# PSUM divided into two two-bank and four one-bank tiles in a packed-attention and squared-ReLU kernel

## The chip, the cores and the metric

The kernel runs on one core of a Trainium2 chip. The metric is the device time of one execution in microseconds (us). The core has five engines that run side by side, each through its own queue in order: TensorE (PE, matrix products), ScalarE (ACT), VectorE (DVE), GpSimd (POOL) and SyncE (SP, which here issues the stores). Matrix products are written into PSUM, an accumulator memory of eight banks; one bank holds 512 fp32 values in each of 128 partitions. ACT and DVE read PSUM and write the results to SBUF. Below, "to evict" a PSUM tile means to copy its values out of PSUM.

## The reference

There are 8 batches of 8 heads, 576 tokens, 64 values a head, and 32 packed queries. The attention is done twice, and its output goes through a feed-forward layer with a squared ReLU:

```
p_packed = softmax(p @ k^T / 8) @ v              # 32 packed rows per head
x        = softmax(q @ p_packed^T / 8) @ p_packed  # 576 rows per head
x        = x of all heads side by side           # (4608, 512)
h        = x @ w_in                              # (4608, 2048)
out      = relu(h)**2 @ w_out                    # (4608, 512), float32
```

## The kernel before

Work is cut by batch b (0 to 7), by quad qd of four heads (0, 1), by block fb of 128 of the 2048 hidden features (0 to 15), and by output tile t of 128 tokens (0 to 35). A batch has 576 tokens, thus four and a half output tiles. The steps of a batch are:

- **S1.b.0 and S1.b.1** (`s1`, L348): first scores of one quad, eight matmuls of 128x128 into one bank, then one exponential on ACT (`s1_exp`, L354). Both quads share one two-bank tile. **S1.b.2** (`s1_rest`, L357) holds what is left of both quads in the first bank of a second tile, `psr`.
- **PV.b.qd** (`pv`, L365): the packed values and the softmax sums, into the second bank of `psr`. **XT.b** (`pq_block`, `recip`, `extract`) takes them out of PSUM in small pieces on DVE and ACT, and only then is `psr` free.
- **M.b** (`m`, L398): the packed values times w_in, with 16 small matmuls for two chunks of 512 features. For b of 1 and above one M step takes two two-bank tiles at once; each is evicted in two pieces, one by ACT (L413) and one by DVE (L415).
- **S2.b.qd** (`s2`, L421): second scores, four matmuls of 288 columns into two banks, exponential on ACT (L431). **N.b.qd** (`n_sum`, L433): their sums, two matmuls, then logarithm and exponential on ACT and a product on DVE (L446).
- **F1.b.fb** (`f1_mm`, L450): four matmuls of 288 columns into a two-bank tile `ps_h`, ReLU on ACT (L465), square on DVE (L471) into `gT`, which holds two batches.
- **F2.t.fb** (`f2_mm`, L479): one matmul of 512 columns per fb, 16 of them accumulated into one bank for output tile t (L483). ACT or DVE then copies the bank to `o_sb` (`f2_out`, L497, helper `cast`, L260 and L262) and SP issues four stores. The even and the odd tile of a pair share one two-bank PSUM tile and one `o_sb` buffer.

The order of all instructions is written out by a planner (`Plan`, L47) that runs when the program is built. It knows the steps, their dependencies, a cost in us for each piece, a delay for a signal between engines (`HOPS`), and pools of slots. Each step takes slots before it starts and gives them back when a named piece ends. It books steps one after the other: the one that can start first goes first, with a small bias by stream, in which F2 comes last and F1 just before it. Each engine then gets its instructions in the order of the planned starts. On the chip, an engine whose next instruction waits does nothing else meanwhile.

The pool that matters is `"ps": 4`, four tiles of two banks, which are all of PSUM. S1, `psr`, M, S2, N, F1 and F2 all take from it. Waits for the tile's former use are put in by the framework when a tile is handed out again under the same tag, and also between instructions that use the same tile. The lines about F2 and its pool:

```
                if fb == 0 and t % 2 == 0:
                    take.append(("ps", 1))
...
                    if t % 2:
                        give.append(("ps", 1, f"F2.{t - 1}.0"))
                        give.append(("osb", 1, f"F2.{t - 1}.{fb}"))
...
                                lag=2.5 if fb == NFB - 1 and t % 2 else 0.0))
```

`lag` adds 2.5 us in the plan to the time at which the slots come free and at which the step counts as done. F1 of batch b depends on the last F2 step of the tiles of batch b - 2, since it writes over their half of `gT`.

Of the kernel before, what the change touches and what calls it, by code (L numbers as in the profile page):

```python
# [18 lines left out]
GM = 4  # L19
# [170 lines left out]
def kernel_impl(tc, q, k, v, p, w_in, w_out, out):  # L190
    nc = tc.nc
    B, H, S, Dh = q.shape
    assert Dh == D and S == JT * 32 and H == 2 * QH
    NQD = H // QH
# [9 lines left out]
    with ExitStack() as ctx:  # L204
# [2 lines left out]
        qkv = ctx.enter_context(tc.tile_pool(name="qkv", bufs=3))  # L207
        small = ctx.enter_context(tc.tile_pool(name="small", bufs=3))
        rpool = ctx.enter_context(tc.tile_pool(name="rpool", bufs=4))
        opool = ctx.enter_context(tc.tile_pool(name="opool", bufs=2))  # L210
        psum = ctx.enter_context(tc.tile_pool(name="psum", bufs=1, space=bass.MemoryType.PSUM))

        nc.scalar.preload_act_table_set("natural_log_exp_and_others")
# [20 lines left out]
        rD = [consts.tile([P, NQD], F32, name=f"rD{i}") for i in range(2)]  # L234
        gT = consts.tile([P, NFB, 2 * S], BF16, name="gT")

        def ps_tile(name, step, i=0):
            ps = psum.tile([P, 2, 512], F32, name=name, tag=f"ps{plan.slot['ps', step][i]}")
            for _ in range(plan.fill):
                nc.tensor.matmul(ps[:, 0, :256], lhsT=idle_b[:, :P], rhs=idle_b, start=True, stop=True)  # L240
            plan.fill = 0
            return ps

# [63 lines left out]
        class Att:  # L307
            def __init__(self, b):
                self.b = b
                self.v, self.vg, self.kT, self.pT, self.pq = v_b[b % NVB], v_g[b % 2], kT[b % NKT], pT_bd[b % NPT], pq_bd[b % 2]  # L310
                self.qT, self.a2, self.M = qT[b % 2], a2[b % 2], M[b % 2]
                self.e1, self.e1r, self.ppT, self.rD = e1[b % 2], e1r[b % 2], ppT[b % 2], rD[b % 2]
                self.kb, self.qb = {}, {}
                self.psm, self.pss, self.psn, self.e2, self.ls = {}, {}, {}, {}, {}

            def load_kq(self, nm, qd):
                t = getattr(self, nm + "b")[qd] = qkv.tile([P, JT * D], BF16, name=nm + "_b")
# [28 lines left out]
                    nc.tensor.matmul(ps, lhsT=kt[:, dh], rhs=self.pT[:, blk(qd, dh)], start=(dh == 0), stop=(dh == 1))  # L346

            def s1(self, qd):  # L348
                if qd == 0:
                    self.ps1 = ps_tile("ps_s1", f"S1.{self.b}.0")  # L350
                for g in range(GM):
                    self.s1_mm(self.ps1[:, qd, g * P:(g + 1) * P], qd, g)

            def s1_exp(self, qd):  # L354
                nc.scalar.activation(self.e1[:, qd], self.ps1[:, qd], ACT.Exp, scale=0.125)  # L355

            def s1_rest(self):  # L357
                self.psr = ps_tile("ps_pp", f"S1.{self.b}.2")
                for qd in range(NQD):
                    self.s1_mm(self.psr[:, 0, qd * P:(qd + 1) * P], qd, GM)  # L360

            def s1_rest_exp(self):
                nc.scalar.activation(self.e1r, self.psr[:, 0, :NQD * P], ACT.Exp, scale=0.125)

            def pv(self, qd):  # L365
                ps = self.ps_pp = self.psr[:, 1]

                def e1(g, i0, i1):
                    return self.e1[:, qd, g, i0:i1] if g < GM else self.e1r[:, qd, i0:i1]

                for pr in range(2):
                    h0 = qd * QH + 2 * pr
                    c0 = qd * P + pr * 64
                    for g in range(GM + 1):
                        nc.tensor.matmul(ps[:, c0:c0 + 64], lhsT=self.vg[:, g, h0 * D:(h0 + 2) * D],  # L375
                                         rhs=e1(g, pr * 64, pr * 64 + 64), start=(g == 0), stop=(g == GM))
# [98 lines left out]
        def tok(t):  # L475
            n0 = (t * P) % (2 * S)
            return slice(n0, n0 + P)

        def f2_mm(t, fb):  # L479
            if fb == 0:  # L480
                if t % 2 == 0:
                    po[t // 2] = ps_tile("ps_o", f"F2.{t}.0")
            nc.tensor.matmul(po[t // 2][:, t % 2], lhsT=gT[:, fb, tok(t)], rhs=w_out_b[:, fb, :],  # L483
                             start=(fb == 0), stop=(fb == NFB - 1))

        def o_tile(s):
            if s not in ob:
                ob[s] = opool.tile([P, 2, NE], F32, name="o_sb")
            return ob[s]

        def store(t, cols=slice(None)):
            for i in range(4):
                b, j = divmod(t * 4 + i, JT)
                dst = out[b * S:(b + 1) * S, :].rearrange("(a j) e -> j a e", j=JT)[j]
                nc.sync.dma_start(dst[:, cols], ob[t // 2][32 * i:32 * i + 32, t % 2, cols])

        def f2_out(t, eng):  # L497
            cast(eng, o_tile(t // 2)[:, t % 2], po[t // 2][:, t % 2])
            store(t)

        V, A, Q = nc.vector, nc.scalar, nc.gpsimd

        plan = Plan({"ps": 4, "kb": 3, "qb": 3, "v": NVB, "e2": 3, "r": 4, "osb": 2, "ls": 3, })
        T = [Att(b) for b in range(B)]
        QDS = range(NQD)
        NDV = 1
# [45 lines left out]
        def s1_steps(b):  # L552
            old = [f"PV.{b - 2}.1"] if b > 1 else []
            return [Step(f"S1.{b}.{qd}", [stage([("PE", 0.45, lambda qd=qd: T[b].s1(qd))]),
                                          stage([("ACT", 0.5, lambda qd=qd: T[b].s1_exp(qd))])],
                         [f"Tk.{b}.{qd}", f"X.{b}"] + old, [("ps", 1)] if qd == 0 else [],
                         [("ps", 1, f"S1.{b}.0")] if qd == NQD - 1 else []) for qd in QDS] + [
                    Step(f"S1.{b}.2", [stage([("PE", 0.23, T[b].s1_rest)]), stage([("ACT", 0.3, T[b].s1_rest_exp)])],
                         [f"Tk.{b}.{qd}" for qd in QDS] + [f"X.{b}"] + old, [("ps", 1)])]

        def pv_steps(b):
            old = [f"S2.{b - 2}.{qd}" for qd in QDS] + [m_of(b - 2, NFB - 1), m_of(b - 2, 0)] if b > 1 else []
# [10 lines left out]
                         [f"PV.{b}.1"] + old, (), [("ps", 1, f"S1.{b}.2")])]  # L573

        def g_steps(b):
            old = [f"PV.{b - 2}.1"] if b > 1 else []
# [5 lines left out]
        def m_steps(b):  # L582
            pairs = [(c,) for c in range(NWC)] if b == 0 else [(0, 1), (2, 3)]
            old = [f"F1.{b - 2}.{NFB - 1}"] if b > 1 else []
            return [Step(f"M.{b}.{cs[0]}",
                         [stage([("PE", 0.22 + 0.215 * len(cs), lambda cs=cs: T[b].m(cs))]),
                          stage(*[[("ACT", 0.6, lambda c=c, qd=qd: T[b].m_out(c, qd, A)),
                                   ("DVE", 0.67, lambda c=c, qd=qd: T[b].m_out(c, qd, V))] for c in cs for qd in QDS])],
                         [f"XT.{b}"] + [f"WI.{c}" for c in cs] + old, [("ps", len(cs))], [("ps", 1, None)])
                    for cs in pairs]  # L590

        def m_of(b, fb):
# [3 lines left out]
        def s2_steps(b):  # L596
            res = []
            for qd in QDS:
                res.append(Step(f"S2.{b}.{qd}", [stage([("PE", 0.49, lambda qd=qd: T[b].s2(qd))]),
                                                 stage([("ACT", 0.64, lambda qd=qd: T[b].s2_exp(qd))])],  # L600
                                [f"XT.{b}/1.{i}" for i in range(3)] + [f"Tq.{b}.{qd}"],
                                [("ps", 1), ("e2", 1)], [("ps", 1, None)]))
                res.append(Step(f"N.{b}.{qd}", [stage([("PE", 0.245, lambda qd=qd: T[b].n_sum(qd))]),
                                                stage([("ACT", 0.55, lambda qd=qd: T[b].n_ln(qd))]),
                                                stage([("ACT", 0.58, lambda qd=qd: T[b].n_inv(qd))]),
                                                stage([("DVE", 0.66, lambda qd=qd: T[b].n_mul(qd))])],
                                [f"S2.{b}.{qd}"] + ([f"F1.{b - 2}.{NFB - 1}"] if b > 1 else []), [("ps", 1), ("ls", 1)],
                                [("ps", 1, None), ("ls", 3, None), ("e2", 3, f"S2.{b}.{qd}")]))
            return [res[0], res[2], res[1], res[3]]

        def last_use(t):
# [4 lines left out]
        def f1_steps(b):  # L616
# [8 lines left out]
                         [("ps", 1), ("r", 1)], [("ps", 1, None), ("r", 2, None)]) for fb in range(NFB)]  # L625

        def f1_of(*ts):
            return sorted({t * P // S for t in ts} | {(t * P + P - 1) // S for t in ts})
# [1 line left out]
        def f2_steps(t):  # L630
            bs = f1_of(t)
            res = []
            for fb in range(NFB):
                segs = [stage([("PE", 0.2158, lambda fb=fb: f2_mm(t, fb))])]
                take, give = [], []
                if fb == 0 and t % 2 == 0:
                    take.append(("ps", 1))
                if fb == NFB - 1:
                    segs.append(stage([("ACT", 0.5, lambda: f2_out(t, A)), ("DVE", 0.59, lambda: f2_out(t, V))]))
                    if t % 2:  # L640
                        give.append(("ps", 1, f"F2.{t - 1}.0"))
# [75 lines left out]
```

## Time and profile before

| What | Value |
|---|---|
| Median of three runs | 283.61 us (283.16 to 284.52) |
| Profiled execution, its own time | 282.97 us |
| Span of its instructions | 281.2 us |
| PE busy | 236.8 us (84%) |
| ACT busy | 162.7 us (58%) |
| DVE busy | 149.9 us (53%) |
| POOL busy | 58.8 us (21%) |
| Granted TensorE clock, mean | 0.998 |
| F2 matmuls (L483) | 132.3 us busy |
| F1 matmuls (L454) | 72.6 us busy |
| M, S2 and N matmuls (L406, L425, L436) | 11.9, 11.4 and 6.2 us busy |
| Stores to `out` | 144 of 64 KB, 1.7 us to landing |

A profile lists when each instruction began and ended. PEld is the loading of weights into TensorE, which lies beside its matmuls. A row "A <- B: 8.4, 13, 0.7" among the waits says that an engine stood idle before instruction group A for 8.4 us in total, 13 times, 0.7 us at the longest, and that B was the last thing that it waited for. In the timeline a row gives start, duration, engine, line, operation, and in brackets the idle time of that engine just before it. Matmuls overlap one another, so the duration of a row of one matmul is longer than the distance between two of them. The profile records a few per cent of matmuls not at all, which makes some counts in rows too small.

### The profile page before, as it was taken

What the parts mean: (1) busy time and instruction counts of PE and PEld (TensorE: products, weight loads), DVE (VectorE), ACT (ScalarE), POOL (GpSimd) and SP (SyncE); (2) the same over time, 40 slices, a digit from 0 to 9 for tenths busy, and PEclk for the clock granted to TensorE, in tenths of its full rate; (3) what the DMA queues carried; (4) which work ended last, traced back from release to release, by engine and by line L of the source; (5) the groups of instructions that cost most, each with busy time, mean ns of one, the idle gap of its engine ahead of it and who ended that gap; (6) DMA issues with size and microseconds to landing.
All of it is one profiled execution on the core that took longest, in us unless ns stands there. A gap on an engine that the chain in (4) does not pass through costs nothing.

```text
span 281.2 us, 4890 instructions
## 1 busy us (share of the span) xinstructions
PE 236.8 (84%) x1812; PEld 134.4 (48%) x1840; DVE 149.9 (53%) x329; ACT 162.7 (58%) x304; POOL 58.8 (21%) x113
## 2 busy tenths in 40 slices
PE   0566688996979898978988998899899998988883
PEld 0523454654645565437633574366337545634341
DVE  5565898989988995557543184236506403700000
ACT  1237798978897655658862396458718515801110
POOL 8932643557467500000000000000000000000000
PEclk9999999999999999999999999999999999999999
DMA  6999999899999991211012200330131122023222
GB/s 94 178 206 208 203 205 196 150 177 158 212 220 222 221 207 53 59 37 40 0 40 65 65 23 1 76 77 0 37 77 37 28 63 61 1 70 80 57 61 69
DMA packets 26615, 28.37 MB, mean 101 GB/s; under 512 B 5600, under 2 KB 17888, under 8 KB 26592
## 3 DMA queue, kind: packets, MB, share of 16 engines
q0 software_dynamic: 19680, 18.62, 41.5%
q1 hardware_dynamic: 6912, 9.45, 13.5%
q8 instruction: 14, 0.23, 0.3%
q14 instruction: 9, 0.07, 0.1%
HBM read 37.22 MB, written 9.44 MB: 166 GB/s over the span
## 4 chain that ended last, share of the span: by engine, by line
PE 68%; DVE 13%; ACT 10%; issue 3%; DMA 3%; POOL 1%; ACTq 0%; DVEq 0%; POOLq 0%
PE ps_o L483 38%; PE ps_h L454 21%; DVE M L415 3%; ACT o_sb L260 3%; ACT M L413 3%; DVE qT L332 2%; PE ps_m L406 2%; DMA v_b<-in_v_dram 2%; PE ps_s L346 2%; PE ps_s L425 2%; PE ps_pp L375 2%; DVE kT L338 2%; DVE a L446 2%; DVE pq_bd L262 1%; ACT ls L443 1%
## 5 line engine op out<-in xcount | busy, mean ns | idle before, releaser
L483 PE MATMUL ps_o<-w_out_b,gT 128*128 128x512 bf16 x548 | 132.3, 379 | 13.8 <-ACT o_sb L260 8.4
L483 PEld LDWEIGHTS <-gT 128*128 128x128 bf16 x576 | 55.0, 98 | 76.3 <-issue 21.8
L471 DVE TENSOR_TENSOR gT<-r 128x576 bf16<-128x576 bf16 x128 | 57.1, 458 | 54.7 <-ACT r L465 47.9
L454 PE MATMUL ps_h<-a,M 128*128 128x288 bf16 x512 | 72.6, 290 | 5.6 <-DVE a L446 2.3
L465 ACT ACTIVATE r<-ps_h 128x576 bf16<-128x576 f32 x126 | 71.8, 676 | 9.4 <-PE ps_h L454 9.2
L454 PEld LDWEIGHTS <-M 128*128 128x128 bf16 x512 | 49.7, 99 | 24.7 <-issue 4.8
L260 ACT COPY o_sb<-ps_o 128x512 f32<-128x512 f32 x32 | 18.8, 587 | 60.6 <-PE ps_o L483 54.8
L413 ACT ACTIVATE M<-ps_m,rD 128x512 bf16<-128x512 f32 x41 | 26.0, 688 | 11.9 <-PE ps_m L406 9.3
L415 DVE TENSOR_SCALAR M<-ps_m,rD 128x512 bf16<-128x512 f32 x23 | 16.6, 747 | 19.4 <-ACT M L413 14.8
L332 DVE STREAM_TRANSPOSE qT<-q_b 128x1152 bf16<-128x1152 bf16 x16 | 21.7, 1366 | 0.5 <-DMA q_b<-in_q_dram 0.4
L323 POOL DMA_DIRECT2D v_b<-in_v_dram x32 | 20.0, 634 | 7.2 <-DMA w_in_b<-in_moe_w_in_dram 3.9
L346 PE MATMUL ps_s<-pT_bd,kT 128*128 128x128 bf16 x128 | 10.4, 230 | 11.5 <-DVE kT L338 9.9
L338 DVE STREAM_TRANSPOSE kT<-k_b 128x320 f32<-128x320 f32 (+1 forms) x32 | 18.7, 681 | 1.4 <-DMA k_b<-in_k_dram 1.3
L346 PEld LDWEIGHTS <-kT 128*128 128x128 bf16 x160 | 10.6, 103 | 15.0 <-DVE kT L338 13.5
L446 DVE TENSOR_TENSOR a<-e,ls 128x576 bf16<-128x576 bf16 x16 | 11.7, 749 | 10.8 <-ACT ls L443 10.7
L425 PE MATMUL ps_s<-qT,pq_bd 128*128 128x288 bf16 x64 | 11.4, 303 | 6.8 <-DVE pq_bd L262 3.7
L355 ACT ACTIVATE e<-ps_s 128x512 bf16<-128x512 f32 x16 | 9.4, 599 | 12.4 <-PE ps_s L346 12.3
L431 ACT ACTIVATE e<-ps_s,rD 128x576 bf16<-128x576 f32 x16 | 11.8, 742 | 6.0 <-PE ps_s L425 5.9
L440 ACT ACTIVATE ls<-ps_n 128x576 f32<-128x576 f32 x16 | 9.9, 648 | 6.1 <-PE ps_n L436 6.1
L406 PE MATMUL ps_m<-w_in_b,ppT 64*32 64x512 bf16 x256 | 11.9, 402 | 0.4 <-DVE M L415 0.2
L425 PEld LDWEIGHTS <-pq_bd 128*128 128x128 bf16 x64 | 6.1, 100 | 12.6 <-issue 4.6
L318 POOL DMA_DIRECT2D k_b<-in_k_dram x16 | 8.6, 544 | 13.5 <-DVE kT L338 10.8
(46 smaller groups left out, 128.5 us busy)
## 6 DMA issues: line engine op xcount, KB each, us to landing
out_dram<-o_sb SPq DMA_DIRECT2D x144, 64.0 KB, 1.7
k_b<-in_k_dram POOLq DMA_DIRECT2D x16, 288.0 KB, 6.6
q_b<-in_q_dram POOLq DMA_DIRECT2D x16, 288.0 KB, 7.4
v_b<-in_v_dram POOLq DMA_DIRECT2D x16, 160.0 KB, 6.4
v_b<-in_v_dram POOLq DMA_DIRECT2D x16, 128.0 KB, 6.6
w_in_b<-in_moe_w_in_dram POOLq DMA_DIRECT2D x4, 512.0 KB, 10.3
w_out_b<-in_moe_w_out_dram POOLq DMA_DIRECT2D x8, 256.0 KB, 9.0
p_b<-in_p_dram POOLq DMA_DIRECT2D x1, 192.0 KB, 10.0
```

The costliest lines, as they stand in the source:

```text
L260: nc.scalar.copy(dst, src)
L323: nc.gpsimd.dma_start(self.v[i:P:4, :, :n * D], v[self.b].rearrange("h (a j) d -> a h (j d)", j=JT)[:, :, J0[i] * D:(J0[i] + n) * D])
L332: nc.vector.transpose(self.qT[:, qd].rearrange("p dh (j a) -> p j dh a", a=32), self.qb[qd][:].rearrange("p (j dh dl) -> p j dh dl", dh=2, ...
L338: nc.vector.transpose(self.kT[:, qd, :n * P].rearrange("p (g a jp) -> p jp g a", jp=4, a=32)[:, i:i + 2], self.kb[qd][:, J0[i] * D:(J0[i] ...
L346: nc.tensor.matmul(ps, lhsT=kt[:, dh], rhs=self.pT[:, blk(qd, dh)], start=(dh == 0), stop=(dh == 1))
L413: nc.scalar.activation(dst, self.psm[c][:, qd], ACT.Copy, scale=self.rD[:, qd:qd + 1])
L415: nc.vector.tensor_scalar_mul(dst, self.psm[c][:, qd], self.rD[:, qd:qd + 1])
L425: nc.tensor.matmul(ps[:, c], lhsT=self.pq[:, blk(qd, dh)], rhs=self.qT[:, qd, dh, c * HALF:(c + 1) * HALF], start=(dh == 0), stop=(dh == 1))
L454: nc.tensor.matmul(ps[:, c], lhsT=a.M[:, qd, fb * FB:(fb + 1) * FB], rhs=a.a2[:, qd, c * HALF:(c + 1) * HALF], start=(qd == 0), stop=(qd = ...
L465: nc.scalar.activation(Att.cols(r), ph[a.b, fb], ACT.Relu)
L471: eng.tensor_tensor(out=g_of(a.b, fb), in0=r, in1=r, op=ALU.mult)
L483: nc.tensor.matmul(po[t // 2][:, t % 2], lhsT=gT[:, fb, tok(t)], rhs=w_out_b[:, fb, :], start=(fb == 0), stop=(fb == NFB - 1))
```

## The change

The pool `ps` of four two-bank tiles becomes two pools: `p2`, two tiles of two banks, and `p1`, four tiles of one bank. M, S2, N and F1 take from `p2`. Each quad of the first scores, `psr` and each output tile take one tile from `p1`. The rest of the first scores and the packed values now lie in the same bank one after the other, where they had a bank each. An M step of two chunks takes both `p2` tiles. Each output tile has its own `o_sb` buffer: four buffers of one tile, where there were two buffers of two. The lag of 2.5 us now stands behind every output tile, and each gives back its slots itself. No costs and no stream priorities are changed, and the planner makes a new order from the new pools.

```diff
-        opool = ctx.enter_context(tc.tile_pool(name="opool", bufs=2))
+        opool = ctx.enter_context(tc.tile_pool(name="opool", bufs=4))
...
-        def ps_tile(name, step, i=0):
-            ps = psum.tile([P, 2, 512], F32, name=name, tag=f"ps{plan.slot['ps', step][i]}")
+        def ps_tile(name, step, i=0, pool="p2"):
+            ps = psum.tile([P, 2, 512] if pool == "p2" else [P, 512], F32, name=name,
+                           tag=f"{pool}_{plan.slot[pool, step][i]}")
...
             def s1(self, qd):
-                if qd == 0:
-                    self.ps1 = ps_tile("ps_s1", f"S1.{self.b}.0")
+                ps = self.ps1[qd] = ps_tile("ps_s1", f"S1.{self.b}.{qd}", pool="p1")
...
             def s1_rest(self):
-                self.psr = ps_tile("ps_pp", f"S1.{self.b}.2")
+                self.psr = ps_tile("ps_pp", f"S1.{self.b}.2", pool="p1")
...
             def pv(self, qd):
-                ps = self.ps_pp = self.psr[:, 1]
+                ps = self.ps_pp = self.psr
...
             if fb == 0:
-                if t % 2 == 0:
-                    po[t // 2] = ps_tile("ps_o", f"F2.{t}.0")
-            nc.tensor.matmul(po[t // 2][:, t % 2], lhsT=gT[:, fb, tok(t)], rhs=w_out_b[:, fb, :],
+                po[t] = ps_tile("ps_o", f"F2.{t}.0", pool="p1")
+            nc.tensor.matmul(po[t], lhsT=gT[:, fb, tok(t)], rhs=w_out_b[:, fb, :],
...
-                ob[s] = opool.tile([P, 2, NE], F32, name="o_sb")
+                ob[s] = opool.tile([P, NE], F32, name="o_sb")
...
-        plan = Plan({"ps": 4, "kb": 3, "qb": 3, "v": NVB, "e2": 3, "r": 4, "osb": 2, "ls": 3, })
+        plan = Plan({"p2": 2, "p1": 4, "kb": 3, "qb": 3, "v": NVB, "e2": 3, "r": 4, "osb": 4, "ls": 3, })
...
-                         [f"XT.{b}"] + [f"WI.{c}" for c in cs] + old, [("ps", len(cs))], [("ps", 1, None)])
+                         [f"XT.{b}"] + [f"WI.{c}" for c in cs] + old, [("p2", len(cs))], [("p2", 1, None)])
...
-                if fb == 0 and t % 2 == 0:
-                    take.append(("ps", 1))
+                if fb == 0:
+                    take.append(("p1", 1))
...
-                    if t % 2:
-                        give.append(("ps", 1, f"F2.{t - 1}.0"))
-                        give.append(("osb", 1, f"F2.{t - 1}.{fb}"))
-                    else:
-                        take.append(("osb", 1))
+                    give += [("p1", 1, f"F2.{t}.0"), ("osb", 1, None)]
+                    take.append(("osb", 1))
...
-                                lag=2.5 if fb == NFB - 1 and t % 2 else 0.0))
+                                lag=2.5 if fb == NFB - 1 else 0.0))
```

More of the change, by code (lines that the diff above doesn't have):

```diff
@@ L235, in kernel_impl @@
         gT = consts.tile([P, NFB, 2 * S], BF16, name="gT")
-        def ps_tile(name, step, i=0):
-            ps = psum.tile([P, 2, 512], F32, name=name, tag=f"ps{plan.slot['ps', step][i]}")
+        def ps_tile(name, step, i=0, pool="p2"):
+            ps = psum.tile([P, 2, 512] if pool == "p2" else [P, 512], F32, name=name,
+                           tag=f"{pool}_{plan.slot[pool, step][i]}")
             for _ in range(plan.fill):
-                nc.tensor.matmul(ps[:, 0, :256], lhsT=idle_b[:, :P], rhs=idle_b, start=True, stop=True)
+                nc.tensor.matmul(ps[:, 0, :256] if pool == "p2" else ps[:, :256], lhsT=idle_b[:, :P], rhs=idle_b, start=True, stop=True)
             plan.fill = 0
@@ L313, in __init__ @@
                 self.kb, self.qb = {}, {}
-                self.psm, self.pss, self.psn, self.e2, self.ls = {}, {}, {}, {}, {}
+                self.psm, self.pss, self.psn, self.e2, self.ps1, self.ls = {}, {}, {}, {}, {}, {}
             def load_kq(self, nm, qd):
@@ L348, in s1 @@
             def s1(self, qd):
-                if qd == 0:
-                    self.ps1 = ps_tile("ps_s1", f"S1.{self.b}.0")
+                ps = self.ps1[qd] = ps_tile("ps_s1", f"S1.{self.b}.{qd}", pool="p1")
                 for g in range(GM):
-                    self.s1_mm(self.ps1[:, qd, g * P:(g + 1) * P], qd, g)
+                    self.s1_mm(ps[:, g * P:(g + 1) * P], qd, g)
             def s1_exp(self, qd):
-                nc.scalar.activation(self.e1[:, qd], self.ps1[:, qd], ACT.Exp, scale=0.125)
+                nc.scalar.activation(self.e1[:, qd], self.ps1[qd], ACT.Exp, scale=0.125)
             def s1_rest(self):
-                self.psr = ps_tile("ps_pp", f"S1.{self.b}.2")
+                self.psr = ps_tile("ps_pp", f"S1.{self.b}.2", pool="p1")
                 for qd in range(NQD):
-                    self.s1_mm(self.psr[:, 0, qd * P:(qd + 1) * P], qd, GM)
+                    self.s1_mm(self.psr[:, qd * P:(qd + 1) * P], qd, GM)
             def s1_rest_exp(self):
-                nc.scalar.activation(self.e1r, self.psr[:, 0, :NQD * P], ACT.Exp, scale=0.125)
+                nc.scalar.activation(self.e1r, self.psr[:, :NQD * P], ACT.Exp, scale=0.125)
             def pv(self, qd):
-                ps = self.ps_pp = self.psr[:, 1]
+                ps = self.ps_pp = self.psr
                 def e1(g, i0, i1):
@@ L494, in store @@
                 dst = out[b * S:(b + 1) * S, :].rearrange("(a j) e -> j a e", j=JT)[j]
-                nc.sync.dma_start(dst[:, cols], ob[t // 2][32 * i:32 * i + 32, t % 2, cols])
+                nc.sync.dma_start(dst[:, cols], ob[t][32 * i:32 * i + 32, cols])
         def f2_out(t, eng):
-            cast(eng, o_tile(t // 2)[:, t % 2], po[t // 2][:, t % 2])
+            cast(eng, o_tile(t), po[t])
             store(t)
         V, A, Q = nc.vector, nc.scalar, nc.gpsimd
-        plan = Plan({"ps": 4, "kb": 3, "qb": 3, "v": NVB, "e2": 3, "r": 4, "osb": 2, "ls": 3, })
+        plan = Plan({"p2": 2, "p1": 4, "kb": 3, "qb": 3, "v": NVB, "e2": 3, "r": 4, "osb": 4, "ls": 3, })
         T = [Att(b) for b in range(B)]
@@ L555, in s1_steps @@
                                           stage([("ACT", 0.5, lambda qd=qd: T[b].s1_exp(qd))])],
-                         [f"Tk.{b}.{qd}", f"X.{b}"] + old, [("ps", 1)] if qd == 0 else [],
-                         [("ps", 1, f"S1.{b}.0")] if qd == NQD - 1 else []) for qd in QDS] + [
+                         [f"Tk.{b}.{qd}", f"X.{b}"] + old, [("p1", 1)], [("p1", 1, None)]) for qd in QDS] + [
                     Step(f"S1.{b}.2", [stage([("PE", 0.23, T[b].s1_rest)]), stage([("ACT", 0.3, T[b].s1_rest_exp)])],
-                         [f"Tk.{b}.{qd}" for qd in QDS] + [f"X.{b}"] + old, [("ps", 1)])]
+                         [f"Tk.{b}.{qd}" for qd in QDS] + [f"X.{b}"] + old, [("p1", 1)])]
         def pv_steps(b):
@@ L572, in pv_steps @@
                                            [("DVE", 0.55, lambda: T[b].extract(V))])],
-                         [f"PV.{b}.1"] + old, (), [("ps", 1, f"S1.{b}.2")])]
+                         [f"PV.{b}.1"] + old, (), [("p1", 1, f"S1.{b}.2")])]
         def g_steps(b):
@@ L601, in s2_steps @@
                                 [f"XT.{b}/1.{i}" for i in range(3)] + [f"Tq.{b}.{qd}"],
-                                [("ps", 1), ("e2", 1)], [("ps", 1, None)]))
+                                [("p2", 1), ("e2", 1)], [("p2", 1, None)]))
                 res.append(Step(f"N.{b}.{qd}", [stage([("PE", 0.245, lambda qd=qd: T[b].n_sum(qd))]),
@@ L606, in s2_steps @@
                                                 stage([("DVE", 0.66, lambda qd=qd: T[b].n_mul(qd))])],
-                                [f"S2.{b}.{qd}"] + ([f"F1.{b - 2}.{NFB - 1}"] if b > 1 else []), [("ps", 1), ("ls", 1)],
-                                [("ps", 1, None), ("ls", 3, None), ("e2", 3, f"S2.{b}.{qd}")]))
+                                [f"S2.{b}.{qd}"] + ([f"F1.{b - 2}.{NFB - 1}"] if b > 1 else []), [("p2", 1), ("ls", 1)],
+                                [("p2", 1, None), ("ls", 3, None), ("e2", 3, f"S2.{b}.{qd}")]))
             return [res[0], res[2], res[1], res[3]]
@@ L624, in f1_steps @@
                          [m_of(b, fb)] + [f"N.{b}.{qd}" for qd in QDS] + old,
-                         [("ps", 1), ("r", 1)], [("ps", 1, None), ("r", 2, None)]) for fb in range(NFB)]
+                         [("p2", 1), ("r", 1)], [("p2", 1, None), ("r", 2, None)]) for fb in range(NFB)]
         def f1_of(*ts):
```

## The prediction

> **What bounds the kernel now.** I read the page first, then the waits of all engines, then the timeline in the stretches that the waits named. The page's slices show PE nearly full from the seventh slice on, and its clock full throughout:
>
> ```profile
> PE   0566688996979898978988998899899998988883
> PEclk9999999999999999999999999999999999999999
> ```
>
> PE is busy 236.8 us of 281.2, so 44 us are idle. The stretches of 10 us put some 20 of them before 50 us, where inputs arrive, and 4.6 behind the last matmul at 276.6 us. About 20 us are spread over the full middle, and the waits name the largest of them:
>
> ```profile
> PE ps_o L483 <- ACT o_sb L260: 8.4, 13, 0.7
> ...
> PE ps_o L483 <- ACT ls L440: 1.6, 1, 1.6
> ...
> PE ps_h L454 <- DVE ppT L262: 1.6, 1, 1.6
> PE ps_o L483 <- DVE M L415: 1.1, 1, 1.1
> PE ps_o L483 <- DVE o_sb L262: 1.0, 1, 1.0
> ```
>
> Fourteen times PE stands still for an output tile's eviction, 8.4 + 1.0 = 9.4 us. The tail, where only F2 is left, shows which tile waits:
>
> ```profile
> 265.44 7.07 PE L483 MATMUL ps_o<-w_out_b,gT 128*128 128x512 bf16 x32 [0.72 <-ACT o_sb L260]
> 268.87 0.59 ACT L260 COPY o_sb<-ps_o 128x512 f32<-128x512 f32 x1 [3.48 <-PE ps_o L483]
> 272.59 0.59 ACT L260 COPY o_sb<-ps_o 128x512 f32<-128x512 f32 x1 [3.13 <-PE ps_o L483]
> 273.22 3.40 PE L483 MATMUL ps_o<-w_out_b,gT 128*128 128x512 bf16 x14 [0.72 <-ACT o_sb L260]
> ```
>
> The last 16 matmuls (14 recorded) are tile 35, and the 32 before them are tiles 33 and 34. Tile 33's copy at 268.87 holds nothing up: tile 34 goes into another PSUM tile. Tile 34's copy at 272.59 stops PE until 273.22, although tile 35 goes into the other bank. So the odd tile waits for the even one because both are one tile to the framework.
>
> The F1 steps run in bursts, and in one stretch singly among F2:
>
> ```profile
> 129.13 7.47 PE L454 MATMUL ps_h<-a,M 128*128 128x288 bf16 x56
> 129.82 7.71 ACT L465 ACTIVATE r<-ps_h 128x576 bf16<-128x576 f32 x14 [0.62 <-PE ps_h L454]
> ```
>
> ```profile
> 103.44 0.65 PE L454 MATMUL ps_h<-a,M 128*128 128x288 bf16 x4
> 103.94 1.24 PE L483 MATMUL ps_o<-w_out_b,gT 128*128 128x512 bf16 x5
> 105.01 0.65 PE L454 MATMUL ps_h<-a,M 128*128 128x288 bf16 x4
> ```
>
> Fourteen steps in 7.47 us are 0.534 us each. In the second stretch (PE busy 9.79 us of 100 to 110) F2 matmuls fill the time between F1 steps with no idle row.
>
> **The output tiles.** With a bank each, tile t + 1 has no part in tile t's eviction. All 14 waits go: -9.4 us. What is late next there is only the slot: a tile's 16 matmuls take 16 x 0.216 = 3.5 us (the row of 32: (7.07 - 0.38) / 31 = 0.216), its copy ends about 0.8 us later, the plan adds 2.5 us, so 6.8 us in all; alone, F2 keeps two of the four `p1` slots. [...]
>
> **Waits across kinds of tile.** F2 waited for N's slot (1.6) and for M's (1.1), F1 for the slot of the packed values (1.6) and for first scores (0.5), first scores for M's and S2's slots (0.4 and 0.3): 5.5 us of waits between steps that no longer share a pool. Bounds 0 and 5.5. I take 4.0, near the upper end, because the three largest are cut by the pools themselves; the small ones can meet another wait.
>
> **F1 with two tiles.** A tile is in use for 0.69 us from first matmul to ReLU (129.13 to 129.82), 0.68 for the ReLU (L465's mean), and about 0.04 until PE goes on (copy ended 272.59 + 0.59, PE began 273.22): 1.41 us. Two tiles give a step per 0.70 us, of which PE works 0.49 to 0.50 (four matmuls, 103.44 until F2 goes on at 103.94). The hole of 0.21 is one F2 matmul. What covers it is F2's backlog. Counted by weight loads in stretches of 20 us, F2 had done 62 at 80 us, 149 at 120, 241 at 160 and 333 at 200, when whole batches finished by F1 had made available 144, 216, 288 and 432 (72 a batch): 47 to 99 matmuls, at least 10 us, in hand; a batch's F1 needs about 16. With cover it costs 0; without any, 128 x (0.70 - 0.534) = 21 us. I take 0 after 45 us, by the stretch at 100 us. Before about 41 us there is no F2, so the first batch's 16 steps are bare: 0 to 16 x 0.17 = 2.7 us, and I take 1.0, since they were already spread over 17 us by other waits. If an F1 step's wait comes late, the F2 matmuls queued behind it on PE wait too.
>
> **M with both tiles.** This is the new wait. One M step now blocks F1, S2 and N:
>
> ```profile
> 143.37 0.62 PE L406 MATMUL ps_m<-w_in_b,ppT 64*32 64x512 bf16 x16
> 143.85 1.27 ACT L413 ACTIVATE M<-ps_m,rD 128x512 bf16<-128x512 f32 x2 [1.06 <-PE ps_m L406]
> ...
> 144.58 1.41 DVE L415 TENSOR_SCALAR M<-ps_m,rD 128x512 bf16<-128x512 f32 x2 [2.69 <-ACT M L413]
> ...
> 146.04 0.63 PE L406 MATMUL ps_m<-w_in_b,ppT 64*32 64x512 bf16 x16 [0.21 <-DVE M L415]
> ```
>
> DVE starts behind ACT's first piece, so the tiles are empty 2.62 us after the first matmul, where the plan's own figures (0.65 + 0.2 + 1.34 + 0.14) say 2.33. Whoever is planned right behind M comes up to 0.3 early and stops PE, with F2 queued behind. There are 14 such steps. The rows of a PE wait on DVE's M are 0.2, 0.3, 0.7 and 1.1 us; bounds 0 and 14 x 1.05 = 14.7. I take the row of the same pair of steps, 0.21: 2.9 us.
>
> **Costs at nothing.** The extra lag holds F1 of batches 2, 3, 6 and 7 (their last awaited tile is even: 4, 8, 22, 26) 2.5 us longer in the plan; the F2 backlog of 10 us covers it, and without that cover it is 10 us. PV now writes the bank that the rest's exponential reads; in the trace it comes after that exponential anyway (127.42 + 0.39, PV at 128.30), bare it is 8 x 0.4. The stores are the same 144; a copy now waits for the stores of one tile, not two, and ACT's 5.8 us of such waits lay beside PE work. Instruction counts on ACT and DVE do not change.
>
> **The clock.** The rows show 1.00 in every stretch, also where F1 and F2 alternate. [...]
> My sum takes full clock.
>
> **The sum.** 282.97 - 9.4 - 4.0 + 1.0 + 2.9 = 273.5 us for the profiled execution. The median of the runs stands 0.6 above it, so 274.0.
>
> **Rivals.**
> - *PE full (0.20):* F2 is never short of a bank and the M waits vanish in filler. 282.97 - 9.4 - 5.5 = 268.1, and if the bursts' excess over 0.49 us a step goes for 50 of 128 steps, another 2. For it: the stretch at 100 us. Against: the M rows. 266 to 270.
> - *Given back (0.10):* M's waits are 0.7 to 1.05 us, 9.8 to 14.7 us instead of 2.9: 280.4 to 285.3. For it: the rows of 0.7 us before S2 and 1.1 before F2. Against: the other two rows of a wait on DVE's M are 0.2 and 0.3.
> - *The two-bank pool becomes the bound, slower (0.10):* the plan lines up F1, M, S2 and N without enough F2 between, and F1 steps wait 0.17 us each. All bare it is 21 us: 273.5 - 1.0 + 21 = 293.5, some 288 if three quarters are. It decides against the change from 10 us on, over half of the steps bare. Against it: per batch the pool is in use for 16 x 0.70 + 2 x 2.62 us + about 3 for S2 and N = 19.5 us, while batches follow one another every 24 to 30 us (bursts at 129, 159, 185, 211 and 235).
> - *The change does not do what it says* (0.03): the odd tile's wait is on something else and stays; then 282.97 - 4 + 3.9, about 283.
>
> **How the numbers follow.** The forecast case, 271 to 278, has 0.57. Range 267 to 283.5: below lies a part of the full-PE case, above lie the slower rival and the worst third of what is given back, 0.18 in all. A measurement of this kernel can tell about 0.5% from no change. Faster by more takes the forecast, full PE and a third of the given-back case: 0.80; within 0.5% 0.07; slower 0.13.
>
> **What would show it.** Right: no row of L483 waiting on `o_sb`; the tail from the last F1 on shorter by 0.7 us per pair of output tiles; F1 bursts gone, with one or two F2 matmuls behind each step or pair; new rows of F1, S2, N or M waiting on DVE or ACT M of 0.2 to 0.3 us; clock 1.00. Wrong: F1 waiting on ACT `r` over 5 us, M's waits over 10, or odd tiles still waiting.

## The result and the profile after

| What | Before | After |
|---|---|---|
| Median of four runs each | 283.8 us | 267.97 us (267.14 to 269.03) |
| Ratio after to before | | 0.9444 (95% interval 0.9403 to 0.9485) |
| Profiled execution, own time | 282.97 us | 267.14 us |
| Span | 281.2 us | 265.4 us |
| PE busy | 236.8 us | 236.8 us |

The kernel became 5.6% faster. The forecast was 274.0 us with a range of 267 to 283.5; the measured time lies at the lower end, in the case called "PE full" (266 to 270 us, chance 0.20), and not in the likeliest case. The range held by 1 us. The profiled executions differ by 15.8 us, and PE's idle time differs by the same: 44.4 us before, 28.6 us after.

The page's slices of the changed kernel, to set beside those of before:

```profile
PE   0547788998996998998999999999999999999993
PEclk9999999999999999999999999999999999999999
```

From the 20th slice on PE is full. The windows of the changed kernel say by how much (the columns are: length, then busy time and instructions of PE, its weight loads, DVE, ACT and POOL, then clock, DMA share, GB/s):

```profile
0.00:50.00 50.00, 31.67 (x277) 18.02 (x278) 34.49 (x83) 28.48 (x52) 27.83 (x51) 1.00 1.18 186
50.00:100.00 50.00, 46.52 (x473) 28.05 (x472) 46.98 (x96) 38.15 (x76) 31.08 (x63) 1.00 1.15 205
...
150.00:200.00 50.00, 49.88 (x345) 27.76 (x344) 24.79 (x51) 35.73 (x60) 0.00 (x0) 1.00 0.20 48
200.00:240.00 40.00, 40.00 (x242) 23.56 (x241) 15.69 (x34) 23.32 (x37) 0.00 (x0) 1.00 0.19 43
```

The first of these stretches before:

```profile
0.00:50.00 50.00, 30.50 (x284) 18.23 (x286) 35.20 (x85) 29.06 (x54) 27.58 (x50) 1.00 1.18 185
```

Before, PE was busy 30.5 us of the first 50 and idle 20.3 us between 50 us and the last matmul. After, it is busy 31.7 us of the first 50, and idle 5.6 us from there to the last matmul. So 14.7 of the 15.8 us come from the middle and the tail, 1.2 from the start.

The tail is now one row of PE, with copies beside it that stop nothing:

```profile
239.66 21.10 PE L482 MATMUL ps_o<-w_out_b,gT 128*128 128x512 bf16 x97
253.93 0.58 ACT L261 COPY o_sb<-ps_o 128x512 f32<-128x512 f32 x1 [2.91 <-PE ps_o L482]
257.38 0.58 ACT L261 COPY o_sb<-ps_o 128x512 f32<-128x512 f32 x1 [2.87 <-PE ps_o L482]
```

Two tiles now take 32 x 0.216 = 6.9 us (the copies are 3.45 apart). Before, the row at 265.44 that the prediction shows and the one ahead of it were 7.79 us apart for the same work:

```profile
257.65 7.07 PE L483 MATMUL ps_o<-w_out_b,gT 128*128 128x512 bf16 x31 [0.72 <-ACT o_sb L260]
```

A pair of output tiles thus cost 0.88 us, more than the 0.67 to 0.72 us of the wait rows, because a matmul's modelled end lies 0.16 us after the start of the next one (0.38 against 0.216) and hides that much of a stop.

That distance also corrects a detail of the reading before. From 265.44, tile 33's copy at 268.87 leaves room for 15 matmuls, not 16 (265.44 + 14 x 0.216 + 0.38 = 268.84). So one matmul of the odd tile goes ahead of the stop, the row at 273.22 is the other 15 (14 recorded), and the even tile's copy waits for that first matmul too: they hold up each other.

The F1 steps of the changed kernel look like the single ones at 100 us before:

```profile
133.13 0.65 PE L454 MATMUL ps_h<-a,M 128*128 128x288 bf16 x4
133.62 0.38 PE L482 MATMUL ps_o<-w_out_b,gT 128*128 128x512 bf16 x1
133.84 0.65 PE L454 MATMUL ps_h<-a,M 128*128 128x288 bf16 x4
134.33 0.38 PE L482 MATMUL ps_o<-w_out_b,gT 128*128 128x512 bf16 x1
```

One step per 0.71 us, with one F2 matmul in the hole, and no idle time.

What is left of PE's waits:

```profile
PE ps_s L347 <- DVE kT L339: 10.4, 4, 7.3
PE ps_s L425 <- DVE qT L333: 2.8, 3, 1.3
...
PE ps_h L454 <- DVE M L415: 1.3, 3, 0.7
...
PE ps_pp L347 <- ACT e L355: 1.1, 1, 1.1
```

There is no row of F2 (L482) among them. The waits on M's evictions lie before 50 us, except one of 0.12 us at 195. After 50 us there remain 2.4 us of first scores waiting for keys (82 to 84.6 us), 2.0 us of first scores waiting for a tile that an exponential still reads (102 and 125 us), and 0.8 us for queries.

### The profile page after: what moved, and what is told of

Same layout as the page of the kernel before. It is cut to its first block, busy times and chain, and to the rows that moved or that the text cites. A ratio compares the mean times of both kernels' runs of the same rounds, so it can differ in the third digit from the quotient of the medians.

```text
span 265.4 us, 4905 instructions
## 1 busy us (share of the span) xinstructions
PE 236.8 (89%) x1840; PEld 134.9 (51%) x1840; DVE 153.1 (58%) x335; ACT 166.5 (63%) x298; POOL 58.9 (22%) x113
## 4 chain that ended last, share of the span: by engine, by line
PE 71%; DVE 12%; ACT 7%; DMA 5%; issue 2%; POOL 1%; DVEq 0%; ACTq 0%; POOLq 0%
PE ps_o L482 41%; PE ps_h L454 20%; DMA v_b<-in_v_dram 4%; PE ps_s L425 3%; DVE M L415 3%; DVE qT L333 2%; PE ps_m L406 2%; DVE pq_bd L263 2%; PE ps_pp L375 2%; DVE kT L339 2%; ACT pq_bd L261 2%; ACT M L413 1%; ACT r L465 1%; PE ps_n L436 1%; PE ps_s L347 1%
## 5 line engine op out<-in xcount | busy, mean ns | idle before, releaser
L482 PE MATMUL ps_o<-w_out_b,gT 128*128 128x512 bf16 x576 | 145.9, 380 | 0.0
L465 ACT ACTIVATE r<-ps_h 128x576 bf16<-128x576 f32 x127 | 80.7, 652 | 13.5 <-PE ps_h L454 9.4
L454 PE MATMUL ps_h<-a,M 128*128 128x288 bf16 x512 | 82.9, 292 | 3.6 <-DVE M L415 1.3
L482 PEld LDWEIGHTS <-gT 128*128 128x128 bf16 x576 | 55.1, 98 | 54.6 <-issue 4.0
L454 PEld LDWEIGHTS <-M 128*128 128x128 bf16 x512 | 50.0, 99 | 28.4 <-issue 4.6
L261 ACT COPY o_sb<-ps_o 128x512 f32<-128x512 f32 x28 | 16.4, 587 | 39.4 <-PE ps_o L482 39.4
L413 ACT ACTIVATE M<-ps_m,rD 128x512 bf16<-128x512 f32 x38 | 24.0, 685 | 10.3 <-PE ps_m L406 9.5
L415 DVE TENSOR_SCALAR M<-ps_m,rD 128x512 bf16<-128x512 f32 x26 | 18.6, 745 | 14.9 <-ACT M L413 11.5
L324 POOL DMA_DIRECT2D v_b<-in_v_dram x32 | 19.0, 609 | 6.5 <-DMA w_in_b<-in_moe_w_in_dram 4.0
L319 POOL DMA_DIRECT2D q_b<-in_q_dram x16 | 9.1, 572 | 11.6 <-DVE qT L333 5.5
```

The costliest lines, as they stand in the source:

```text
L261: nc.scalar.copy(dst, src)
L324: nc.gpsimd.dma_start(self.v[i:P:4, :, :n * D], v[self.b].rearrange("h (a j) d -> a h (j d)", j=JT)[:, :, J0[i] * D:(J0[i] + n) * D])
L413: nc.scalar.activation(dst, self.psm[c][:, qd], ACT.Copy, scale=self.rD[:, qd:qd + 1])
L415: nc.vector.tensor_scalar_mul(dst, self.psm[c][:, qd], self.rD[:, qd:qd + 1])
L454: nc.tensor.matmul(ps[:, c], lhsT=a.M[:, qd, fb * FB:(fb + 1) * FB], rhs=a.a2[:, qd, c * HALF:(c + 1) * HALF], start=(qd == 0), stop=(qd = ...
L465: nc.scalar.activation(Att.cols(r), ph[a.b, fb], ACT.Relu)
```

## The experiments

Theory A was the prediction's: the odd tile's wait is worth its rows, the waits between kinds of tile are worth a few us more, and F2 covers what the short two-bank pool costs. The rivals are named with each run.

**The wait alone, put back.** In the changed kernel, in its own order, a matmul of one column with zero weights reads what the even tile's copy wrote, ahead of the odd tile's next matmul:

```diff
+            if t % 2 and t - 1 in evicted and t not in waited:
+                waited.add(t)
+                nc.tensor.matmul(po[t][:, :1], lhsT=idle_b[:, :P], rhs=ob[t - 1][:, :1].bitcast(BF16)[:, 1:2],
+                                 start=(fb == 0), stop=(fb == 0))
...
+            evicted.add(t)
```

> The changed kernel in its own order, with the wait of the odd output tile put back alone: ahead of the first matmul of an odd tile that comes after the even tile's copy in the order, a matmul of one column with zero weights reads a value that this copy wrote. 18 such matmuls are added (under 0.1 us each). Theory A (the wait itself was worth 9.4 us in whatever order): each of the 18 odd tiles waits up to 0.67 to 0.72 us again, so 268.0 + 9 to 13 = 277 to 281 us. Theory B (the gain came from the new order of steps, and the waits would now fall on time that is free anyway): at most 272 us.

Measured: 275.95 us (ratio to before 0.9739, 0.9706 to 0.9771), 8.0 us above the changed kernel. That is 1 us under theory A's range and far from the rival's. The trace of this run shows a stop:

```profile
252.51 0.16 PE L484 MATMUL ps_o<-o_sb,idle_b 128*128 128x1 bf16 x1 [0.46 <-ACT o_sb L261]
252.54 7.07 PE L486 MATMUL ps_o<-w_out_b,gT 128*128 128x512 bf16 x32
260.06 0.16 PE L484 MATMUL ps_o<-o_sb,idle_b 128*128 128x1 bf16 x1 [0.46 <-ACT o_sb L261]
```

The pair period is 7.55 us (252.51 to 260.06), 0.64 over 6.91, not 0.88: here the copy does not wait for the odd tile's first matmul, only the other way round. That is still within the 0.5 to 0.72 us that theory A took for each. What falls short is the count: of the 18 added matmuls only 10 have a row of waiting (6 behind ACT's copies, 4 behind DVE's), since at most of the others different work already lay between. Ten stops of 0.64 make some 6.4 of the 8.0 us; the rest was not traced (the profiled execution also has a stretch at half clock, see the last section). The new order does not make the wait free.

**The output tiles alone.** The kernel before, with two one-bank tiles for F2 and three two-bank tiles for all the rest:

```diff
-        plan = Plan({"ps": 4, ...
+        plan = Plan({"ps": 3, "po": 2, ...
...
+                po[t] = ps_tile("ps_o", f"F2.{t}.0", pool="po")
```

> The kernel before with the output tiles alone taken out of the shared pool: two one-bank tiles for F2, three two-bank tiles for all the rest, first scores and packed values included. Theory A: the odd tile's waits (9.4) and F2's waits for the slots of N and M (2.7) go, the waits between first scores, packed values, F1 and M stay: 283.8 - 12.1 = 271.7, within 269.5 to 274 us. Theory B (it takes both divisions, since two-bank tiles kept by the packed values hold up F1 and M): above 275 us.

Measured: 266.05 us (0.9383, 0.9351 to 0.9416), 5.7 us below theory A's 271.7 and outside its range. This part alone brings 17.7 us, more than the whole change. Its PE waits after 50 us sum to 3.7 us; one of 1.2 us of F1 behind the packed values stayed. The expectation had taken only F2's own waits (12.1 us) off.

**The first scores and packed values alone.** Two one-bank tiles for them; F2 keeps its pairs and shares three two-bank tiles with M, S2, N and F1:

```diff
-        plan = Plan({"p2": 2, "p1": 4, ...
+        plan = Plan({"p2": 3, "p1": 2, ...
...
-                po[t] = ps_tile("ps_o", f"F2.{t}.0", pool="p1")
+                if t % 2 == 0:
+                    po[t // 2] = ps_tile("ps_o", f"F2.{t}.0")
```

> The other part alone: first scores and packed values have two one-bank tiles of their own; F2 keeps its pairs in a shared two-bank tile and takes them from the three two-bank tiles that M, S2, N and F1 use. Theory A: the odd tile's 9.4 us stay, only waits of F1 and the first scores (up to 2.8) go, and F2 can still be short of a tile: 283.8 - 2.8 + 0 to 3 = 280 to 285 us. Theory B: most of the gain is here, below 275 us.

Measured: 282.26 us (0.995, 0.9925 to 0.9976), 1.5 us below before, within theory A's range. Its waits are those of before:

```profile
PE ps_o L483 <- ACT o_sb L261: 7.8, 14, 0.7
...
PE ps_o L483 <- DVE M L415: 1.6, 2, 1.0
PE ps_o L483 <- ACT ls L440: 1.6, 1, 1.6
```

So nearly all of the gain comes with the output tiles: F2's pair wait, its waits for a tile that N or M still held, and what the new order brings besides.

**One tile over two banks.** To tell the tile from the bank, the kernel with the output tiles alone keeps its order and its two banks, but both banks are one tile made once:

```diff
-                po[t] = ps_tile("ps_o", f"F2.{t}.0", pool="po")
+                if not big:
+                    big.append(psum.tile([P, 2, 512], F32, name="ps_o"))
+                po[t] = big[0][:, plan.slot["po", f"F2.{t}.0"][0]]
```

> The kernel with the output tiles alone divided off, in the same order and in the same two banks, but both banks belong to one tile that is made once, so that output tiles alternate between its halves. Theory A (instructions are kept apart by tile and not by bank; each boundary between two output tiles costs PE 0.86 us, which is what a pair in the tail of the kernel before took over 32 x 0.216 us): 35 boundaries x 0.86 = 30 us at most, less where other work lies between: 266.0 + 24 to 30 = 290 to 296 us. Rival (the wait comes from the bank or from the slot, or from something else that one tile does not bring back): 265.5 to 267 us. If the price of a boundary is the 0.67 us of the wait rows: 266 + 23 = 289 us at most.

Measured: 286.35 us (1.0099, 1.0075 to 1.0123); the same kernel with two tiles ran beside it at 265.18. So 21.2 us, under the 24 to 30 expected, and far from the rival. The tail:

```profile
251.30 3.61 PE L483 MATMUL ps_o<-w_out_b,gT 128*128 128x512 bf16 x16 [0.67 <-ACT o_sb L259]
254.95 0.58 ACT L259 COPY o_sb<-ps_o 128x512 f32<-128x512 f32 x1 [3.70 <-PE ps_o L483]
255.59 3.61 PE L483 MATMUL ps_o<-w_out_b,gT 128*128 128x512 bf16 x16 [0.67 <-ACT o_sb L259]
```

Each tile takes 4.29 us where 16 x 0.216 = 3.45 would do: 0.84 us a boundary. The waits list 27 stops, not 35 (22 behind ACT's copies, 5 behind DVE's); 21.2 / 27 = 0.79 each. At the other eight boundaries other matmuls lay between. That settles the cause of the stops: the order is the same in both kernels, neighbouring output tiles lie in different banks in both, and the stop comes with the shared tile.

**F1 with a longer claim on its tiles.** The planner is told that an F1 tile comes free 0.7 us later:

```diff
-                         [("p2", 1), ("r", 1)], [("p2", 1, None), ("r", 2, None)]) for fb in range(NFB)]
+                         [("p2", 1), ("r", 1)], [("p2", 1, None), ("r", 2, None)], lag=0.7) for fb in range(NFB)]
```

> The changed kernel, with the planner told that an F1 tile comes free 0.7 us later than it does (and counts as done that much later), so that two tiles give one F1 step per 1.05 us in the plan and not per 0.70. Theory A (F2 covers the holes; a batch needs 16 x 1.05 + 5.2 for M + 3 for S2 and N = 25 us of the two-bank pool, while PE work of a batch is about 28 us by 223 us / 8): 268 to 272 us. Theory of the two-bank pool as the bound (the slower rival of the prediction): 128 x 0.35 = 45 us more, 300 us and above; a part of it, over 275 us, would say that the pool is near the bound.

Measured: 275.16 us (0.9709, 0.966 to 0.9757), 7.2 us slower than the changed kernel. That is above theory A's range and just over the 275 us from which the expectation would take the pool to be near its bound; the bare price would be 45 us, so F2 covered most of it, but not all. The loss has a place. In the stretch from 76 to 90 us this run's PE first stands idle and then runs at half clock:

```profile
82.00:84.00 2.00, 0.39 (x4) 0.39 (x5) 1.97 (x6) 0.27 (x1) 1.80 (x4) 0.59 1.10 207
84.00:86.00 2.00, 2.00 (x16) 1.63 (x14) 2.00 (x5) 0.87 (x2) 0.68 (x3) 0.50 1.11 208
86.00:88.00 2.00, 2.00 (x34) 1.64 (x32) 2.00 (x3) 0.65 (x1) 1.54 (x4) 0.50 1.31 197
```

Between the two profiled executions (273.70 and 267.14 us) lie 6.6 us. From 76 to 90 us PE idles 1.9 us longer than in the changed kernel, and the lower clock from 84 to 90 us (0.71 in the last two) costs, as an estimate from the windows, 2 x (0.50 + 0.50 + 0.29) = 2.6 us: 4.5 us in all. (At 0.50 an F2 matmul held PE 0.42 us, 85.83 to 86.25, against 0.216 at 1.00.) That the pool is short there (2.1 us a tile in the plan for 1.4) is not shown. The rows of PE's stops in this stretch name keys (2.77 us) and ACT's evictions of M (1.17 and 0.52), not an F1 tile. So the run shows that the new plan is slower, but not that the pool is its limit.

**The plan's 2.5 us behind each output tile.** Taken out, in the changed kernel:

```diff
-                                lag=2.5 if fb == NFB - 1 else 0.0))
+                                lag=0.0))
```

> The changed kernel without the plan's extra 2.5 us behind each output tile (the prediction costed this lag at nothing). Its profile shows two waits of the first scores' rest for a one-bank tile still read by an exponential (0.88 and 1.14 us), while the plan held up to two of the four tiles for output tiles whose copies had ended. Theory A (F2 covers, the lag costs nothing but those waits): 268.0 - 0 to 2 = 266 to 268 us. Rival (the lag holds back F1 of batches 2, 3, 6 and 7 by 2.5 us each, and that is what the changed kernel lacks against the one with the output tiles alone): 264.5 to 266 us.

Measured: 268.51 us (0.9473, 0.9452 to 0.9494): no gain, and 0.5 us above theory A's range. The two waits of the first scores that it was to remove stayed (0.93 and 1.14 us). The lag costs nothing that can be measured, as predicted. In the kernel with the output tiles alone:

> The kernel before with the output tiles alone divided off (three two-bank and two one-bank tiles, 266.05 us), without the plan's lag of 2.5 us behind an output tile. With the lag an output tile holds its bank for 6.8 us, and two banks just carry one tile per 3.46 us. Theory A (two banks are enough with the lag): 265.5 to 266.5 us. Rival (F2 is at the edge of its two banks, and is held back when F1 or M come between): 263 to 265 us.

Measured: 265.74 us (0.9373, 0.9346 to 0.9399): the same again. Two banks carry F2 with the lag.

**M chunk by chunk**, so that no M step takes two tiles:

```diff
-            pairs = [(c,) for c in range(NWC)] if b == 0 else [(0, 1), (2, 3)]
+            pairs = [(c,) for c in range(NWC)]
...
-            return f"M.{b}.{c if b == 0 else c // 2 * 2}"
+            return f"M.{b}.{c}"
```

> The changed kernel with M done chunk by chunk in every batch, so that no M step takes both two-bank tiles. Theory A (F2 fills the time in which M holds both tiles; after 50 us the changed kernel's PE waits on M's eviction for 1.0 us in all): 267 to 269 us, no gain. Rival (M with both tiles is what the two-bank pool of two costs against that of three, 1.9 us): 265.5 to 266.5 us.

Measured: 272.19 us (0.9616, 0.9591 to 0.9642), 4.2 us slower than the changed kernel. (Of the 1.0 us of waits that the expectation puts after 50 us, only 0.12 lie there; 0.87 lie at 46 to 47 us.) And with the output tiles alone:

> The kernel before with the output tiles alone divided off, and M done chunk by chunk in every batch. Theory A: M's pairs cost nothing with three two-bank tiles either, 265 to 267 us. Rival (taking two of three tiles at once holds up F1 and the scores): 263 to 265 us.

Measured: 272.95 us (0.9628, 0.9604 to 0.9652), 7 us slower than without. Both theories failed on the sign. The trace of the first shows a price of the groups themselves, beginning with two rows of the changed kernel, as it was:

```profile
117.98 0.63 PE L406 MATMUL ps_m<-w_in_b,ppT 64*32 64x512 bf16 x16
118.54 2.98 PE L482 MATMUL ps_o<-w_out_b,gT 128*128 128x512 bf16 x13
```

The same work in this run:

```profile
118.98 0.41 PE L406 MATMUL ps_m<-w_in_b,ppT 64*32 64x512 bf16 x8 [0.15 <-DVE M L415]
119.32 0.60 PE L482 MATMUL ps_o<-w_out_b,gT 128*128 128x512 bf16 x2
119.86 0.41 PE L406 MATMUL ps_m<-w_in_b,ppT 64*32 64x512 bf16 x8
120.20 0.39 PE L482 MATMUL ps_o<-w_out_b,gT 128*128 128x512 bf16 x1
120.98 0.41 PE L406 MATMUL ps_m<-w_in_b,ppT 64*32 64x512 bf16 x8 [0.39 <-DVE M L415]
```

Eight M matmuls hold PE 0.34 us until F2 goes on, where sixteen in the changed kernel hold it 0.56 (117.98 to 118.54): 0.12 us more for the same work. Two F2 matmuls ahead of M take 0.54 instead of 0.43: 0.11 more. Fourteen more groups cost, as an estimate from these two, 14 x 0.23 = 3.2 us, and new idle rows behind DVE's evictions (0.15 and 0.39 us here) add to it. The rows name 64*32 for M's matmuls and 128*128 for F2's; what takes the 0.11 to 0.12 us at each change between the two is not shown. M's pair of tiles is thus worth keeping. That the larger loss of the second kernel has the same cause was not traced.

**The two best kernels side by side.**

> The changed kernel once more, beside the next one: 267.1 to 269.0 us, as before.

> The kernel with the output tiles alone divided off once more, beside the changed kernel. Theory A (the rest of the change, two two-bank tiles and not three, gains nothing and costs a little before 110 us): 265.3 to 266.7 us, 0.5 to 1% below the changed kernel. Rival (the difference was one of chips): the same as the changed kernel within 0.3%.

Measured on one chip: 268.27 us (0.947, 0.9437 to 0.9502) for the changed kernel and 265.18 us (0.9343, 0.9319 to 0.9367) for the one with the output tiles alone. The intervals do not meet: the rest of the change costs 3.1 us, a little more than expected. The two profiled executions are 2.3 us apart. Up to 80 us PE is busy 60.4 and 60.7 us, from 110 to 240 us 128.7 and 128.6; between 80 and 110 us the changed kernel's PE is busy 26.6 of 30 us (12.48 + 14.12 in two windows), the other's 28.4 (13.47 + 14.91).

**Whose tile is missing there?** The changed kernel, with its four one-bank tiles divided, two for F2 and two for first scores and packed values:

```diff
-                po[t] = ps_tile("ps_o", f"F2.{t}.0", pool="p1")
+                po[t] = ps_tile("ps_o", f"F2.{t}.0", pool="po")
...
-        plan = Plan({"p2": 2, "p1": 4, ...
+        plan = Plan({"p2": 2, "p1": 2, "po": 2, ...
```

> The changed kernel with its four one-bank tiles divided: two for the output tiles alone, two for the first scores and the packed values alone; two two-bank tiles as in the changed kernel. It tells what the changed kernel lacks (some 2 us between 80 and 106 us) against the one with the output tiles alone and three two-bank tiles. Theory A (it lacks the third two-bank tile): 267 to 269 us, as the changed kernel. Rival (it is the sharing of one-bank tiles between output tiles and first scores, whose rest waited 0.88 and 1.14 us for such a tile): 265 to 266.5 us.

Measured: 267.63 us (0.9457, 0.9431 to 0.9484), as the changed kernel, with PE busy 26.6 of the 30 us again. So sharing the one-bank tiles is not what costs; the third two-bank tile is what is left as a difference between this kernel and the faster one, together with the place of the first scores. Which wait in that stretch follows from it was not separated: between 80 and 110 us the changed kernel's PE waits for keys (2.4 us) and for a tile that an exponential still reads (0.9), PE of the kernel with the output tiles alone once before second scores (1.3), and the orders differ.

## Why the prediction was right, and where its sum was off

The account that came true is that of the rival "PE full": F2 never short of a bank, M's waits vanishing in filler, 268.1 us for the profiled execution against 267.1. The forecast named the same wait and the same cover, but three of its terms were too pessimistic. All three errors went the same way, so that the time lies only 1 us inside the range.

**Right: the wait and its cause.** The sum's largest term, 9.4 us for the odd tiles, is gone with no row left, and the run with one tile over two banks shows that tile and not bank causes it. By experiment it is worth 8.0 us in a weaker form, and 0.79 to 0.88 us a stop in its full form; 14 stops make 11 to 12 us. The rows alone, 0.67 each, undercount.

**Right: F2 covers F1.** Two tiles do give a step per 0.71 us, as worked out (0.70), and the hole holds one F2 matmul. With one and a half times the claim on the tiles the kernel is 7.2 us slower, far from the 45 us of bare steps. That this is the beginning of the rival "the two-bank pool becomes the bound" is not shown.

**Mis-sized: what M's claim on both tiles costs.** The sum took +2.9 us from the row of M after M. After 50 us the trace has 0.12 us of idle time (0.31 us by distance: 0.87 from the first matmul of that M step until F2 goes on, against 0.56). Before 50 us, where F2 has only four matmuls between batch 1's two M steps, the wait did come:

```profile
46.69 0.41 PE L406 MATMUL ps_m<-w_in_b,ppT 64*32 64x512 bf16 x8 [0.62 <-DVE M L415]
```

The step's second half waited 0.25 us more. So the term of 2.9 us measured 1.0 in idle rows. The step that failed is "whoever is planned right behind M comes up to 0.3 early": F2 lies behind M in the order (13 matmuls at 118.54, 11 at 192.12), and the evictions end beside it. Cover by F2 was granted to F1 and should have been granted to M.

**Mis-sized: the start.** It was put at +1.0 us for bare F1 steps. That cost came: F1 waits three times for its own ReLU in the first 50 us, 1.2 us in all, where before it had no such row. Yet PE's idle time in the first 50 us fell by 1.2, with M's 0.87 included, because other waits shrank more: first scores wait 8.0 us for keys there, where they waited 9.9, and F1 waits 2.3 us for its inputs, where it waited 3.2. The sum had no term for these.

**Mis-sized: waits across kinds of tile.** Taken as 4.0 of 5.5 us. All of the rows named are gone. With the 0.87 us of M's wait left in the start, the three terms make 2.8 + 2.2 + 1.5 = 6.5 us, about the whole distance of 6.4 between the sum (273.5) and the profiled execution (267.1).

**The account in rows.** Of 20.3 us idle in the middle, 9.4 + 5.5 named ones are gone, 5.4 should be left, and 5.6 are. But they are not the same ones. Of the 5.4 us, 2.2 were no idle time: the profile before lacks 28 of the 576 F2 matmuls (it has 548, and all 576 weight loads), and its trace has 28 short gaps of PE, 0.01 to 0.17 us, without a releaser; the profile after has all 576. These 2.2 us offset what the idle rows hide of the stops, 14 x 0.16 = 2.2 us. The other 3.2 us are gone too, but for 0.1, and the 5.6 us after are new: keys 2.4, a tile under an exponential 2.0, queries 0.8, and small ones. So the term of the output tiles was some 2.2 us short as well, and about as much came back in waits that had no term.

**Not foreseen: the parts.** The prediction took the change as one. The output tiles alone bring 17.7 to 18.4 us, the first scores alone 1.5, the whole change 15.3 to 15.8: a third two-bank tile, with the first scores in the same pool, is worth some 3 us more here than banks of their own for the first scores. The clock, which the sum took as full, read 1.00 in each stretch of the changed kernel's windows up to 240 us, those with F1 and F2 in turn among them, and 0.97 behind that.

## What to carry to other kernels

When an engine waits on a PSUM tile, look at which tile object it shares and not only at which bank: here two banks in one tile cost 21.2 us, 0.79 at each of 27 hand-overs, and with the same two banks as two tiles the 97 F2 matmuls of the tail ran in one row. Give the work that fills holes buffers of its own first, since a filler that can be starved fills nothing; it can then cover shortages elsewhere, within limits. Here that brought 17.7 us, of which the stops alone make 11 to 12 by the price above; no run parts the two. Price a stop by the distance between equal points of repeated work, with and without it, since the idle row undercounts when matmuls overlap (here 0.67 to 0.72 us in the row, 0.84 to 0.88 by distance).

## What was not expected of the hardware

The TensorE clock fell to half inside the busy middle of some runs. In the run with the longer F1 claim, PE had been idle 2.77 us (80.84 to 83.61) after a stretch that was itself less than half busy (1.74 of the 4 us from 78 to 82), and the clock read 0.50 from 84 to 88 us. In the run with the first scores alone it read 0.68 from 80 to 84 us, where PE was busy 2.38 of 4 us, and 0.89 in the next four. In the run with the wait put back, a wait of 2.19 us at the same place was followed by 0.50 between 88 and 90 us. In the changed kernel's profile the same wait of 2.18 us left the clock at 1.00. So one wait of 2.2 us was followed by half clock in one execution and not in another; what sets the clock is not shown. The spread between executions of the changed kernel (267.1 to 270.5 us over ten runs) may come from this: the three slowest have a mean clock of 0.992 or 0.993, the other seven 0.997 to 0.999. It was not tested, and the kernel before shows no such order (0.992 in a run of 283.19 us, 1.0 in one of 284.38).
